# Attention's main loop given out as tasks by a list schedule, and k's parts carried across the rows by one transfer per head

## The chip, the cores and the metric

One core of a Trainium2 chip runs the whole program. The metric is the device time of one execution in microseconds. Its engines are PE (matmuls, with the weight loads shown apart as PEld), DVE (elementwise and reductions), ACT (activations and copies), POOL, and SP, which here only issues transfers.

## The reference

Attention with talking heads over 4 batches, 12 heads, 448 positions and 64 columns, then a mixture of experts (8 experts, one for each token) and an MLP with h * cos(h). The change touches attention alone:

```python
scores = scale * np.matmul(q, k.transpose(0, 1, 3, 2))
scores = np.einsum('bhij,hg->bgij', scores, w_pre)
scores = scores - np.max(scores, axis=-1, keepdims=True)
attn = np.exp(scores)
attn = attn / (np.sum(attn, axis=-1, keepdims=True) + 1e-09)
attn = np.einsum('bhij,hg->bgij', attn, w_post)
return np.matmul(attn, v)
```

All inputs are float32, and w_in and w_out of the MLP arrive as 64-bit words that the program turns into float32 itself.

## The kernel before

Attention walks over 4 batches. Each batch has 4 chunks of rows (120, 120, 120 and 88), so there are 16 chunks X. A chunk is cut into 12 or 9 blocks, 180 blocks n in all, 45 for each batch. A block holds up to 10 rows with all 12 heads, one row and head to a partition.

For each chunk and head, `qk` makes a score with two matmuls (L170 and L171: k's high part and low part against qs, which has q's high part in one half of the rows and its low part in the other). The scores go from PSUM to a tile S (L43 is the copy on ACT, L45 the one on DVE). For each block, `relay` has SP bring its rows out of S into a tile x (L191). `premix` multiplies x by the mixing matrix kpre into m (L196), DVE takes the row maximum nm (L198) and ACT the exponential E with its sum (L201). `scale` is three short DVE operations (L210, L211, L213) that give kr, the second mixing matrix divided by the sums. `postmix` is four matmuls of E against kr into pa (L223), which is copied to AT. When a chunk is complete, `av` multiplies AT by v (L237, px, copied to xc), `rows` transposes the result (L296, pt, copied to xr, stored by SP), and every fourth chunk or so the gate's logits (L266) and the routing's counts (L568 to L596) follow.

While a batch runs, the heads of the next one are prepared: `load_qk` loads k and q, `turned` transposes a pair of heads on PE (L89), `split_k1` and `split_q1` take the high part on ACT (L100, L121) and the low part on DVE (L101, L122). Scores read k's parts from all 128 rows, but a head's transpose fills only 64 of them. So `split_k1` copies them across: the high part on POOL (L102), the low part on POOL for batch 0 (L104) and on DVE for the others (L106).

Beside this runs the side job `narrow64`: 64 pieces of w_in and w_out. A piece is loaded by SP (L1313, W), squared on ACT (L1317, sq), put together by four DVE operations (L1322 to L1325, f) and stored by SP (L1328). Only the MLP at the end of the program reads the results.

The loop over blocks states the work in one order; which copy goes to ACT and which to DVE is decided by `Balance`, which adds up estimated costs. The order in which each engine and SP then run the loop's instructions is not the written one: outside a `manual_schedule` the compiler's own scheduler orders them by its priorities and its cost model. Each engine runs its instructions strictly in the order that results. Behind the loop, `between` works off the last chunk's products beside the first expert, in a written order.

Of the kernel before, what the change touches and what calls it, by code (L numbers as in the profile page):

```python
# [11 lines left out]
F32 = mybir.dt.float32  # L12
F32R = mybir.dt.float32r
# [14 lines left out]
ROUTE = (1, 8)  # L28
# [3 lines left out]
class Balance:  # L32
# [6 lines left out]
    def copy(self, out, in_, n):  # L39
        a, d = 0.19 + n * 0.00083, 0.07 + n * 0.00104  # L40
        if self.act + a <= self.dve + d:
            self.act += a
            return self.nc.scalar.copy(out, in_)  # L43
        self.dve += d
        return self.nc.vector.tensor_copy(out, in_)  # L45


def attention(ctx, qctx, tc, q, k, v, w_pre, w_post, wg, xs, lg, ident, nb=4, side=None, route=None):
# [45 lines left out]
    def split_k1(b, j, i, ps):  # L94

        h = 2 * j + i
        kh = ok.tile([128, S], F32R, tag=f"KH{h}", name=f"KH{b}_{h}")
        kl = ok.tile([128, S], F32R, tag=f"KL{h}", name=f"KL{b}_{h}")
        r, o = HALF[i], HALF[1 - i]
        nc.scalar.copy(kh[r], ps[r, :S])  # L100
        nc.vector.tensor_tensor(kl[r], ps[r, :S], kh[r].bitcast(F32), op=ALU.subtract)  # L101
        nc.gpsimd.tensor_scalar(kh[o], kh[r].bitcast(F32), 1.0, 0.0, op0=ALU.mult, op1=ALU.add)  # L102
        if b == 0:
            nc.gpsimd.tensor_scalar(kl[o], kl[r].bitcast(F32), 1.0, 0.0, op0=ALU.mult, op1=ALU.add)  # L104
# [258 lines left out]
    for n in range(3):  # L363
        relay(n)
    nxt = [1, 0]
    for n in range(N + 2):
        if n < N:
            X, be = blocks[n]
            b, c = chunks[X]
            nblk = CH[c][2]  # L370
            if n + 3 < N:
                relay(n + 3)

            if X + 1 < len(chunks):
                due = min(H, math.ceil(H * (be + 1) / (nblk - 3)))
                while nxt[0] == X + 1 and nxt[1] < due:
                    qk(X + 1, nxt[1])
                    nxt[1] += 1
                if nxt[0] == X + 1 and be == nblk - 1:
                    nxt = [X + 2, 0]  # L380
            premix(n)

            if b + 1 < nb:
                turn = (c - 2) * 12 + be - 2
                if c == 1 and be in (6, 7, 8):
                    load_qk(b + 1, be - 6)
                for j in range(H):
                    if turn == j * 5 // 4:
                        (split_q if j % 2 else split_k)(b + 1, j // 2)
                        if j in (1, 3, 5):  # L390
                            load_qk(b + 1, j // 2 + 3)
            if be == 2 and X > 0:
                av(X - 1)
            if route is not None and be in ROUTE:
                route.step()
            if be == 3 and c == 0 and X > 0:
                for g in range(4):
                    load_v(b, g)
            if be == 4 and X > 0:
                rows(X - 1)  # L400
            if be == 5 and X - 1 in GROUPS:
                logits_out(GROUPS[X - 1], logits_mm(GROUPS[X - 1]))
            if be == 6 and X - 1 in GROUPS:
                logit_tiles(X - 1)
        if n >= 2:
            postmix(n - 2)
        if n < N:
            scale(n)
        if side is not None:
            side()  # L410
            bal.dve += 0.6
            bal.act += 0.17
    if side is not None:
        side(True)
    if route is not None:
        route.step(True)
# [6 lines left out]
E = 8  # L423
# [867 lines left out]
def narrow64(ctx, tc, pairs, nblocks, bal=None):  # L1291
# [27 lines left out]
    def bits(i):  # L1319
        w, sq = W.pop(i), SQ.pop(i)  # L1320
        f = F[i] = wk.tile([P, C], I32, tag="f", name=f"f{i}")
        V.tensor_scalar(f, w[:, :, 1], 3, 0x3FFFFFFF, op0=ALU.logical_shift_left, op1=ALU.bitwise_and)  # L1322
        V.scalar_tensor_tensor(f, w[:, :, 0], 29, f, op0=ALU.logical_shift_right, op1=ALU.bitwise_or)
        V.scalar_tensor_tensor(f, w[:, :, 1], -0x40000000, f, op0=ALU.bitwise_and, op1=ALU.bitwise_or)
        V.scalar_tensor_tensor(f.bitcast(F32), sq, lim * lim, f.bitcast(F32), op0=ALU.is_ge, op1=ALU.mult)  # L1325
# [4 lines left out]
    stages = (store, bits, square, load)  # L1330
    state = [0, 0.0]

    def step(rest=False):
        state[1] += len(jobs) / nblocks
        while rest or state[1] >= 1:
            state[1] -= 1
            i = state[0]
            if i >= len(jobs) + 3:
                return
            for s, f in enumerate(stages):  # L1340
                j = i - (3 - s)
                if 0 <= j < len(jobs):
                    f(j)
            state[0] += 1

    return step
# [42 lines left out]
def kernel(ctx, tc, q, k, v, w_pre, w_post, w_gate, w1, w2, w_in, w_out, out):  # L1389
# [13 lines left out]
    with ExitStack() as cm:  # L1403
        with ExitStack() as c:
            with ExitStack() as cq:
                side = narrow64(c, tc, [(w_in, wi), (w_out, wo)], 170)
# [116 lines left out]
```

## Time and profile before

| | us |
|---|---|
| three timed runs | 1382.6, 1384.67, 1386.79 |
| median | 1384.67 |
| profiled execution, its own time | 1385.57 |
| its span, first to last instruction | 1383.9 |
| PE busy | 1325.9 |
| DVE busy | 1107.6 |
| ACT busy | 862.8 |
| POOL busy | 105.4 |

Matmuls are pipelined, and the profile models their ends, so the end of one overlaps the start of the next; start to start is the safer measure. In the tables of stretches each row gives the stretch, its length, then for PE, PEld, DVE, ACT and POOL the busy time with the number of instructions, the granted clock of PE as a share of full speed, the busy share of the 16 DMA engines and GB/s. In the lists of groups a row gives line, engine, operation, output<-input with their sizes and the count, then the busy time and the mean ns of one, then the idle time before them and what ended it. In the lists of waits a row gives who waited for whom, the total in us, how often, and the longest. In timelines: start, length, engine, line, operation, count.

### The profile page before, as it was taken

Reading aid. Unit: us, or ns where it says so; the run is one execution under the profiler, and the core shown is the slowest. Engines: PE = TensorE matmul, PEld = TensorE weight load, DVE = VectorE, ACT = ScalarE, POOL = GpSimd, SP = SyncE. Lnnn points to the kernel's source line nnn. Section 1 sums busy time; section 2 is a strip of 40 time slices with the busy share of each in tenths; the row PEclk is TensorE's granted clock in tenths of the full one; section 3 lists DMA queues with packets and bytes.
Section 4 is the critical chain, followed back from the end, with each engine's and each line's share of the span. In section 5 each row is a group of like instructions: output and inputs, shape, how many; then the busy total and the mean of one; then the engine's idle time right before and its main releaser. Section 6 shows DMA issues by size and latency. Waiting matters only on the chain.

```text
span 1383.9 us, 24811 instructions
## 1 busy us (share of the span) xinstructions
PE 1325.9 (96%) x8634; PEld 1103.8 (80%) x8634; DVE 1107.6 (80%) x2529; ACT 862.8 (62%) x1598; POOL 105.4 (8%) x127
## 2 busy tenths in 40 slices
PE   7888999899989999899999999999999999999997
PEld 5666777577767777789999999999888888888886
DVE  8789888998897766899999999899666666666663
ACT  7558656765685555788888888876444444444432
POOL 4001000100010000110001000001100010001001
PEclk9999999999999999999999999999999999999999
DMA  7866666676664337137835876166433343324201
GB/s 191 240 197 197 210 199 211 185 211 211 196 195 133 99 118 268 45 126 274 308 129 164 291 261 217 55 223 210 142 103 114 103 137 103 103 92 138 91 23 46
DMA packets 153281, 227.00 MB, mean 164 GB/s; under 512 B 55744, under 2 KB 115392, under 8 KB 153152
## 3 DMA queue, kind: packets, MB, share of 16 engines
q1 hardware_dynamic: 146816, 200.20, 45.9%
q0 software_dynamic: 3744, 18.09, 3.9%
q10 hardware_dynamic: 2592, 7.08, 1.3%
q8 instruction: 70, 1.15, 0.4%
q14 instruction: 59, 0.48, 0.1%
HBM read 217.87 MB, written 31.85 MB: 180 GB/s over the span
## 4 chain that ended last, share of the span: by engine, by line
PE 57%; issue 0%; DVE 0%; POOLq 0%; ACT 0%; POOL 0%
PE dh L1255 17%; PE op L1199 17%; PE yp L1014 10%; PE h L980 10%; PE ph L1001 1%; PE px L908 1%; PE dpt L1136 1%; POOLq L1518 0%; POOL out_dram L1208 0%; ACT dhs L1259 0%; ACT r L1222 0%; PE gspg L757 0%; DVE r L1220 0%; DVE r L1219 0%; PE pc L793 0%
## 5 line engine op out<-in xcount | busy, mean ns | idle before, releaser
L820 DVE TENSOR_TENSOR wl<-r,wh 128x768 fp32r<-128x768 f32 (+1 forms) x246 | 249.0, 1061 | 12.3 <-ACT wh L819 9.4
L819 ACT CAST wh<-r 128x768 fp32r<-128x768 f32 (+1 forms) x246 | 224.1, 931 | 38.4 <-PE h L980 30.2
L223 PEld LDWEIGHTS pa<-kr,E 120*112 120x112 f32 (+1 forms) x1440 | 168.6, 177 | 59.1 <-issue 26.5
L223 PE MATMUL pa<-kr,E 120*112 120x120 f32 (+1 forms) x1440 | 185.7, 270 | 9.0 <-DVE kr L213 5.6
L196 PE MATMUL m<-x,kpre 120*120 120x448 f32 x360 | 167.2, 548 | 7.0 <-ACT E L201 7.0
L820 DVE TENSOR_TENSOR wil<-wi,wih 128x768 fp32r<-128x768 f32 x64 | 60.9, 953 | 133.9 <-ACT wih L819 133.9
L201 ACT ACTIVATE E<-m,nm 120x448 f32<-120x448 f32 x180 | 114.1, 634 | 70.0 <-DVE nm L198 50.6
L819 ACT CAST wih<-wi 128x768 fp32r<-128x768 f32 x64 | 53.7, 841 | 158.9 <-PE dh L1255 158.0
L198 DVE TENSOR_REDUCE nm<-m 120x1 f32<-120x448 f32 x180 | 110.8, 616 | 9.5 <-PE m L196 8.5
L1199 PE MATMUL op<-woh,gh 128*128 128x512 f32 x448 | 115.2, 338 | 0.0
L1199 PE MATMUL op<-woh,gl 128*128 128x512 f32 x448 | 114.6, 336 | 0.0
L1199 PE MATMUL op<-wol,gh 128*128 128x512 f32 x448 | 114.4, 336 | 0.0
L1255 PE MATMUL dh<-dxh,wih 128*128 128x512 f32 (+1 forms) x384 | 112.8, 369 | 0.0
L1255 PE MATMUL dh<-dxl,wih 128*128 128x512 f32 (+1 forms) x384 | 112.4, 367 | 0.0
L1255 PE MATMUL dh<-dxh,wil 128*128 128x512 f32 (+1 forms) x384 | 111.6, 367 | 0.0
L170 PE MATMUL s<-KH,QS 128*120 128x448 f32 (+1 forms) x192 | 87.6, 456 | 13.0 <-DVE S L45 4.9
L819 ACT CAST woh<-wo 128x768 fp32r<-128x768 f32 x64 | 53.3, 834 | 53.4 <-PE op L1199 51.8
L237 PEld LDWEIGHTS px<-AT,vn 112*64 112x64 f32 x1536 | 75.2, 137 | 8.8 <-ACT AT L43 5.8
L237 PE MATMUL px<-AT,vn 112*64 112x120 f32 (+1 forms) x1536 | 80.9, 261 | 1.1 <-ACT AT L43 0.9
L43 ACT COPY S<-s 120x448 f32<-120x448 f32 (+1 forms) x147 | 75.6, 530 | 9.6 <-PE s L171 8.9
L1255 PEld LDWEIGHTS dh<-dxl,wih 128*128 128x128 f32 x384 | 70.2, 189 | 13.1
L1255 PEld LDWEIGHTS dh<-dxh,wil 128*128 128x128 f32 x384 | 69.8, 189 | 13.1
(263 smaller groups left out, 2723.7 us busy)
## 6 DMA issues: line engine op xcount, KB each, us to landing
r<-in_moe_w_dram SPq DMA_DIRECT2D x54, 1024.0 KB
r<-in_moe_w_dram SPq DMA_DIRECT2D x72, 768.0 KB
x<-S SPq DMA_DIRECT2D x172, 210.0 KB
wi<-wi SPq DMA_DIRECT2D x32, 768.0 KB
wo<-wo SPq DMA_DIRECT2D x32, 768.0 KB
W<-in_moe_w_in_dram SPq DMA_DIRECT2D x32, 384.0 KB
W<-in_moe_w_out_dram SPq DMA_DIRECT2D x32, 384.0 KB
ys<-y ACTq DMA_DIRECT2D x17, 384.0 KB
```

Source lines behind the costliest of these rows:

```text
L170: nc.tensor.matmul(ps[:n, :S], QS[b, h][:, i0 : i0 + n], KH[b, h], start=True, stop=False)
L196: nc.tensor.matmul(ps[:M, :S], kpre[:M, :M], XR.pop(n)[:M], start=True, stop=True)
L198: nc.vector.reduce_max(nm[:M], ps[:M, :S], axis=AX.X, negate=True)
L201: last["act"] = nc.scalar.activation(e[:M], ps[:M, :S], AF.Exp, bias=nm[:M], scale=1.0, accum_out=sg[:M])
L223: nc.tensor.matmul(pa[:112, c, :120], e[:M, c * 112 : c * 112 + 112], kr[:M], start=True, stop=True)
L237: nc.tensor.matmul(px[64 * e : 64 * e + 64, pr, :n], VN[b, g // 3][:, g % 3, cc], AT[X][:, cc, g, :n], start=(cc == 0), stop=(cc == 3))
L819: self.latest["A"] = nc.scalar.copy(hi, src).ins
L820: self.latest["V"] = nc.vector.tensor_tensor(lo, src, hi.bitcast(F32), op=ALU.subtract).ins
L980: self.nc.tensor.matmul(hp[n], a[:, k], w[:, n * 512 : n * 512 + 512], start=(k == 0 and i == 0), stop=(k == 5 and i == 2))
L1014: self.nc.tensor.matmul(yp[n][:, :384], a[:, k], w[:, n * 384 : n * 384 + 384], start=(k == 0 and i == 0), stop=(k == 7 and i == 2))
L1199: nc.tensor.matmul(bank[:, to], g[:, t * P : t * P + P], w[:, of], start=first, stop=(f == 15 and i == 2), skip_group_check=(n == 1))
L1255: nc.tensor.matmul(hp[:, :N], w[:, k], x[:, k, :N], start=(k == 0 and i == 0), stop=(k == 5 and i == 2))
```

## The change

The loop over blocks is gone. Its work is written as tasks, Python generators that yield a step at a time: which engine it runs on and for how long (two numbers: how long the engine is held, how long until the result is there), which buffers it takes and gives back, and which events of other tasks it waits for. A task is a block, the score of a chunk and head, a pair of heads of k or of q, the loads of v, the products of a chunk, the logits of a group with their routing, or a piece of the side job. Each has a rank. `Plan.run` takes, again and again, the step that can start first, and among steps of the same engine that can start within 0.02 us the one of the lowest rank, and emits its instructions at once. A copy that may run on either engine is offered on both. The pieces of the side job are marked `bg`: one is passed over where a step that is not goes first, and their ranks are spread over the loop from 4 to 171 in steps of 170/64. The durations in the steps are numbers like those of a trace. All of it stands in a `manual_schedule` that includes SP, so each engine and SP keep the order in which the plan emitted.

The scores of a batch's last chunk are given a rank 8 blocks earlier than those of others.

k's parts are now the two halves of one tile K of 128 x 2 x 448. For the batches behind the first, POOL issues one transfer per head that copies the 64 rows of both parts to the other 64 rows; POOL's copy of the high part and DVE's copy of the low part (L106) are gone. Batch 0 still has POOL's two copies.

```diff
-        kh = ok.tile([128, S], F32R, tag=f"KH{h}", name=f"KH{b}_{h}")
-        kl = ok.tile([128, S], F32R, tag=f"KL{h}", name=f"KL{b}_{h}")
+        both = ok.tile([128, 2, S], F32R, tag=f"K{h}", name=f"K{b}_{h}")
+        kh, kl = both[:, 0], both[:, 1]
...
-            nc.vector.tensor_copy(kl[o], kl[r].bitcast(F32))
-            bal.dve += 0.3
+            nc.gpsimd.dma_start(out=both[o], in_=both[r])
...
-    for n in range(N + 2):
...
+    def dve(d):
+        return {"DVE": (d - 0.07, d)}
+    def copying(n):
+        return {"ACT": (0.05 + n * 0.00092, 0.12 + n * 0.00092), "DVE": (n * 0.00124, 0.07 + n * 0.00124)}
...
+    def block(n):
+        yield dict(run=dma(4.2), take=["x"], on=[("S", X, h) for h in range(H)], ends=[("x", n)])
+        relay(n)
+        yield dict(run=pe(0.752), take=["m"], reached=n)
...
+        yield dict(run=pe(0.82), later=0.5, take=["o"] + (["AT"] if be == 0 else []), on=[("post", n - 1)] if n else [], ends=[("post", n)])
...
+    for n in range(N):
+        plan.add(n, block(n))
+    for X in range(1, len(chunks)):
+        n0, nb0 = first_of[X], CH[chunks[X - 1][1]][2]
+        for h in range(H):
+            plan.add(n0 - 3 - 8 * (X % 4 == 3) - (H - 1 - h) * (nb0 - 4) / H, score(X, h))
...
+    if side is not None:
+        count, *ops = side
+        for i in range(count):
+            plan.add(4 + i * 170 / count, piece(i, *ops), bg=True)
+    with tc.manual_schedule(engines=START | {mybir.EngineType.SP}):
+        plan.run()
```

What this does to DVE's order is seen near the end of batch one, where heads of the next batch are prepared. Before (L106 is the copy of k's low part, L1324 and L1325 are operations of the side job, L198, L210, L211 and L213 the block's maximum and scaling, L101 and L122 the low parts of k and q):

```order
L211 RECIPROCAL rs_1800<-rs_1800 120x1
L1324 SCALAR_TENSOR_TENSOR f_2529<-W_2289,f_2529 128x384
L106 CAST KL_8_1783<-KL_8_1783 64x448
L101 TENSOR_TENSOR KL_9_1789<-tp_4_0_0_1777,KH_9_1788 64x448
L213 TENSOR_SCALAR kr_1803<-kpost,rs_1800 120x120
L106 CAST KL_9_1789<-KL_9_1789 64x448
L210 TENSOR_SCALAR rs_1839<-sg_1820 120x1
L198 TENSOR_REDUCE nm_1866<-m_1864 120x1
L211 RECIPROCAL rs_1839<-rs_1839 120x1
L1325 SCALAR_TENSOR_TENSOR f_2529<-sq_2422,f_2529 128x384
L122 TENSOR_TENSOR QS_8_1827<-tp_4_1_0_1822,QS_8_1827 64x448
L213 TENSOR_SCALAR kr_1842<-kpost,rs_1839 120x120
```

Now, at the same work (L487 is the maximum, L494, L496 and L499 the scaling, L546 and L555 the low parts, L1563 the side job's first operation):

```order
L487 TENSOR_REDUCE nm_1713<-m_1673 120x1
L496 RECIPROCAL rs_1711<-rs_1711 120x1
L494 TENSOR_SCALAR rs_1719<-sg_1682 120x1
L555 TENSOR_TENSOR QS_6_1715<-tp_3_1_0_1703,QS_6_1715 64x448
L499 TENSOR_SCALAR kr_1727<-kpost,rs_1711 120x120
L496 RECIPROCAL rs_1719<-rs_1719 120x1
L487 TENSOR_REDUCE nm_1734<-m_1695 120x1
L555 TENSOR_TENSOR QS_7_1729<-tp_3_1_0_1703,QS_7_1729 64x448
L499 TENSOR_SCALAR kr_1746<-kpost,rs_1719 120x120
L546 TENSOR_TENSOR K_7_1744<-tp_3_0_0_1661,K_7_1744 64x448
L494 TENSOR_SCALAR rs_1766<-sg_1722 120x1
L1563 TENSOR_SCALAR f_1750<-W_1679 128x384
```

The copies L106 are gone, and the side job's operations stand further apart.

On PE the second place is the border before the third chunk of batch three, from its last score (s_11) on. Before:

```order
L171 MATMUL s_11_4788<-KL_11_3724,QS_11_3819 120x448
L196 MATMUL m_4792<-x_4688,kpre 120x448
L568 LDWEIGHTS tri
L568 MATMUL pq_4810<-ohb,tri 128x8
L570 LDWEIGHTS ones
L570 MATMUL pq_4810<-ohs,ones 128x8
L223 MATMUL pa_4827<-kr_4744,E_4726 112x120 x4
L196 MATMUL m_4840<-x_4712,kpre 120x448
L223 MATMUL pa_4847<-kr_4784,E_4766 112x120 x4
L196 MATMUL m_4870<-x_4756,kpre 120x448
L223 MATMUL pa_4877<-kr_4836,E_4796 112x120
L596 LDWEIGHTS Le_4821
```

There follow a premix, two scores and a postmix before the first premix that reads the new chunk. Now, from the same score:

```order
L522 MATMUL s_11_4843<-K_11_3825,QS_11_3712 120x448
L523 MATMUL s_11_4843<-K_11_3825,QS_11_3712 120x448
L505 MATMUL pa_4847<-kr_4840,E_4818 112x120 x4
L522 MATMUL s_5_4853<-K_5_3518,QS_5_3487 88x448
L523 MATMUL s_5_4853<-K_5_3518,QS_5_3487 88x448
L484 MATMUL m_4859<-x_4690,kpre 120x448
L522 MATMUL s_6_4864<-K_6_3554,QS_6_3515 88x448
L523 MATMUL s_6_4864<-K_6_3554,QS_6_3515 88x448
L484 MATMUL m_4874<-x_4713,kpre 120x448
L522 MATMUL s_7_4882<-K_7_3645,QS_7_3528 88x448
L523 MATMUL s_7_4882<-K_7_3645,QS_7_3528 88x448
L181 MATMUL tp_0_0_0_4888<-ident,kn_0_3772 128x112 x4
```

One more score follows, then the first premix of the new chunk. Scores of the batch's last chunk (of 88 rows) and transposes for the next batch have come in between, and less work lies between the last score and that premix.

## Rows read from the trace of the kernel before

**Rows 1.** The page: engines over the span, PE's 40 slices, an issue of POOL.

```profile
PE 1325.9 (96%) x8634; PEld 1103.8 (80%) x8634; DVE 1107.6 (80%) x2529; ACT 862.8 (62%) x1598; POOL 105.4 (8%) x127
...
PE   7888999899989999899999999999999999999997
...
wpp<-in_w_pre_dram POOLq DMA_DIRECT2D x1, 0.6 KB, 3.2
```

**Rows 2.** Instructions on tile x: durations min/median/max, first and last start.

```profile
L196 PE MATMUL m<-x,kpre x360: 537/539/954, 28.6 to 553.0; 120*120 120x448 f32 x172, 108*108 108x448 f32 x8
L191 SPq DMA_DIRECT2D x<-S x180: 768/801/1127, 24.2 to 543.2; - x180
```

**Rows 3.** Stretches: the four batches and the whole main loop.

```profile
28.60:161.20 132.60, 118.70 (x883) 88.32 (x882) 116.12 (x330) 89.12 (x212) 7.07 (x12) 0.99 0.69 206
161.20:301.90 140.70, 128.59 (x1063) 98.06 (x1062) 125.84 (x384) 89.73 (x215) 7.69 (x12) 0.99 0.69 204
301.90:437.50 135.60, 127.37 (x1068) 96.71 (x1067) 120.72 (x383) 89.57 (x213) 7.27 (x12) 1.00 0.62 189
437.50:557.10 119.60, 118.25 (x1053) 91.78 (x1052) 79.96 (x317) 65.54 (x165) 1.27 (x2) 1.00 0.50 163
28.60:557.10 528.50, 492.90 (x4062) 374.88 (x4061) 442.64 (x1412) 333.96 (x803) 23.31 (x38) 0.99 0.63 191
```

**Rows 4.** Timeline of PE in three short stretches.

```profile
501.64 0.92 PE L196 MATMUL m<-x,kpre 120*120 120x448 f32 x2
502.39 0.98 PE L223 MATMUL pa<-kr,E 120*112 120x120 f32 x8
503.14 0.44 PE L170 MATMUL s<-KH,QS 128*88 128x448 f32 x1
...
503.62 0.92 PE L196 MATMUL m<-x,kpre 120*120 120x448 f32 x2
...
296.90 0.98 PE L223 MATMUL pa<-kr,E 120*112 120x120 f32 x8
297.72 0.92 PE L196 MATMUL m<-x,kpre 108*108 108x448 f32 x2
...
263.76 0.57 PE L89 MATMUL tp<-ident,kn 112*128 112x112 f32 x4 [0.60 <-PE tp L89]
264.18 1.00 PE L223 MATMUL pa<-kr,E 120*112 120x120 f32 x8
```

**Rows 5.** Groups of instructions in the main loop, 28.6 to 557.1 us.

```profile
L237 PE MATMUL px<-AT,vn 112*64 112x120 f32 (+1 forms) x1440 | 77.0, 262 | 1.0 <-ACT AT L43 0.9
L296 PE MATMUL pt<-ident,xc 128*120 128x128 f32 (+1 forms) x90 | 13.0, 278 | 0.0
L266 PE MATMUL pl<-xc,wgs 128*8 128x120 f32 (+1 forms) x180 | 7.0, 261 | 0.0
...
L43 ACT COPY S<-s 120x448 f32<-120x448 f32 (+1 forms) x146 | 75.1, 530 | 9.6 <-PE s L171 8.9
L106 DVE CAST KL<-KL 64x448 fp32r<-64x448 f32 x36 | 14.3, 398 | 1.1
```

**Rows 6.** Waits in the main loop.

```profile
ACT E L201 <- DVE nm L198: 50.6, 67, 4.1
ACT sq L1317 <- DMA W<-in_moe_w_in_dram: 27.5, 18, 3.1
...
PE m L196 <- ACT E L201: 7.0, 11, 1.0
```

**Rows 7.** The same stretches, DVE's operations on tile f alone.

```profile
28.60:161.20 132.60, 44.83 (x90) 0.99 0.69 206
...
437.50:557.10 119.60, 0.00 (x0) 1.00 0.50 163
sum 528.50, DVE 128.22; mean DVE 32.06
```

**Rows 8.** Waits of SP's queue in the main loop.

```profile
SPq L1313 <- DVE f L1324: 41.8, 26, 3.2
```

More of the change, by code (lines that the diff above doesn't have):

```diff
@@ L362, in attention @@
     N = len(blocks)
-    for n in range(3):
-        relay(n)
-    nxt = [1, 0]
-    for n in range(N + 2):
-        if n < N:
-            X, be = blocks[n]
-            b, c = chunks[X]
[L370 to L412, printed above, removed]
@@ L413, in attention, with pe, act @@
-    if side is not None:
-        side(True)
-    if route is not None:
-        route.step(True)
+    first_of = {X: n for n, (X, be) in reversed(list(enumerate(blocks)))}
+    end_of = {X: n for n, (X, be) in enumerate(blocks)}
+    A, V, G = nc.scalar.copy, nc.vector.tensor_copy, nc.gpsimd
+    by = {"ACT": A, "DVE": V}
+    def pe(d):
+        return {"PE": (d, d + 0.17)}
+    def dve(d):
+        return {"DVE": (d - 0.07, d)}
+    def act(d):
+        return {"ACT": (d - 0.07, d)}
+    def copying(n):
+        return {"ACT": (0.05 + n * 0.00092, 0.12 + n * 0.00092), "DVE": (n * 0.00124, 0.07 + n * 0.00124)}
@@ new lines, in score @@
+    def score(X, h):
+        b, c = chunks[X]
+        i0, rows_, _ = CH[c]
+        on = [("K", b, h), ("Q", b, h)]
+        if X >= 2:
+            on += [("x", k) for k in range(first_of[X - 2], end_of[X - 2] + 1)]
+        if h:
+            on.append(("s", X, h - 1))
+        yield dict(run=pe(0.46), take=["q"], on=on, ends=[("s", X, h)])
+        if h == 0:
+            SB[X] = sk.tile([120, H, S], F32, tag="Sb", name=f"S{X}")
+        ps = pq.tile([128, 512], F32, tag="q", name=f"s{X}_{h}")
+        nc.tensor.matmul(ps[:rows_, :S], QS[b, h][:, i0 : i0 + rows_], KH[b, h], start=True, stop=False)
+        nc.tensor.matmul(ps[:rows_, :S], QS[b, h][:, i0 : i0 + rows_], KL[b, h], start=False, stop=True)
+        eng = yield dict(run=copying(S), later=-2, give=["q"], ends=[("S", X, h)])
+        by[eng](SB[X][:rows_, h], ps[:rows_, :S])
@@ new lines, in values, with products @@
+    def values(b):
+        for g in range(4):
+            yield dict(run=dma(3.5), on=[("av", 4 * b - 1, 0), ("av", 4 * b - 1, 1)], ends=[("V", b)] if g == 3 else [])
+            load_v(b, g)
+    def products(X):
+        n = CH[chunks[X][1]][1]
+        b = chunks[X][0]
+        ats = [("AT", k) for k in range(first_of[X], end_of[X] + 1)]
+        for half in range(2):
+            yield dict(run=pe(0.02 * n + 0.21), on=ats + [("V", b)], take=["v"] + (["xc"] if half == 0 else []), give=["AT"] if half else [], ends=[("av", X, half)])
+            px = av_mm(X, half)
+            eng = yield dict(run=copying(3 * n), give=["v"], ends=[("xc", X)] if half else [])
+            av_out(X, half, px, by[eng])
+        for half in range(2):
+            yield dict(run=pe(0.33), take=["v"] + (["xr"] if half == 0 else []))
+            pt = rows_mm(X, half)
+            eng = yield dict(run=copying(384), give=["v"])
+            rows_out(X, half, pt, by[eng])
+        yield dict(run={"none": (0.0, 3.0)}, give=["xr"])
@@ L417, in attention @@
+    for X in range(len(chunks) - 1):
+        plan.add(end_of[X] + 3, products(X))
+    for last_, Xs in GROUPS.items():
+        plan.add(end_of[last_] + 5, gates(Xs))
+        for X in Xs:
+            plan.add(end_of[last_] + 5, freed(X))
+    if side is not None:
+        count, *ops = side
[3 more added lines that the diff above has]
+        plan.run()
     return SimpleNamespace(
@@ L1288, in run, with narrow64 @@
                 part2(item, tiles)
-def narrow64(ctx, tc, pairs, nblocks, bal=None):
+def narrow64(ctx, tc, pairs):
     nc = tc.nc
```

210 lines of the change are left out of this document (189 added, 21 removed).

## The prediction

> **What bounds the kernel now.** First the page's engine shares and slices: PE is busy for 96% of the span, with 7 to 9 tenths up to the eighteenth slice and 9 behind it [rows 1], so a change pays only where PE idles, in the first part. The loose stretch is attention's main loop, from the first premix at 28.6 us [rows 2] to 557.1, its 180 blocks in four batches of 45. The table of stretches cuts it at the batches' first premixes [rows 3]. Batches one to three take 132.6, 140.7 and 135.6 us, with DVE busy for 116 to 126 of each and PE idle for 8 to 14. Batch four takes 119.6, with DVE at 80.0 and PE at 118.2. The granted clock is 0.99 to 1.00 throughout and is no part of this.
>
> How much of PE's busy time is work? The timeline of PE gives start to start, free of the modelled ends [rows 4]: premix 0.75 (501.64 to 502.39), postmix 0.75 before a score (502.39 to 503.14) and 0.82 before a premix (296.90 to 297.72), the two matmuls of a score 0.48 (503.14 to 503.62), four turned pieces 0.42 (263.76 to 264.18). So 180 premixes are 135 us, 180 postmixes at 0.785 (half of each kind, my assumption) 141, 177 scores 85, 36 turns 15; the products with v 77.0, their transposes 13.0 and the logits 7.0 by their busy time [rows 5], and the routing about 10 (an estimate: 13 tiles with four short matmuls each, at most 52 by the 0.278 of a transpose). The sum is 483 us of work in 528.5, or 91%. Batch four alone: 45 blocks 69, 36 scores 17, four of the window's 15 products 20.5, a quarter of transposes, logits and routing 7.5: 114 of 119.6, or 95%. Batches one to three are the other 369 in 408.9, or 90%. That gap is what a better order can win, and the chip has already run the better rate in batch four.
>
> Who is late? In the waits [rows 6] the exponentials on ACT wait 50.6 us for the row maxima of DVE, and ACT stands 27.5 us before squares of the side job whose W has not landed. PE itself waits most for ACT's exponentials, which hold the banks of the premix. Cause: DVE carries the side job early. Its operations on f take 128.2 us, 44.8 of them in batch one and none in batch four [rows 7].
>
> **The change part by part.**
> 1. The copy of k's low part on DVE goes: 36 of 398 ns, 14.3 us [rows 5], all in batches one to three. So do 36 POOL copies of k's high part; POOL is busy for 23.3 of the 528.5 us [rows 3] and heads are made long before they are read, so I count 0 for them.
> 2. In their place POOL issues 36 transfers of both parts. The trace has no such transfer; the nearest POOL row is w_pre, which lands 3.2 us after its issue, but with 0.6 KB [rows 1]; the nearest in size is x, 210 KB against 224, which is issued at 24.2 us and used at 28.6, so at most 4.4 us [rows 2]. In the new order some 14 us of PE's work (7 postmixes, 4 premixes, 11 scores) lie between the last head's transfer (K_11) and its score, and more for the other heads. From either row the price is 0; with the cover gone, each us of lateness would cost up to 1 us for each of 3 batches, as the last head alone is late. Its 8 MB more go beside a DMA share of 0.50 to 0.69 [rows 3]; price 0, at worst what rival 4 has.
> 3. The side job's pieces are spread over the loop. In the new order of DVE 16, 17, 17 and 14 pieces lie in the four batches, against about 22.4, 20.9, 20.9 (the mean of what is left) and 0. A piece is 128.2/64 = 2.0 us. With step 1, a third of it each, DVE goes to about 116.1-4.8-12.8 = 98, 125.8-4.8-7.8 = 113, 120.7-4.8-7.8 = 108, and 80.0+28 = 108. Early, DVE then has slack; in batch four it has 108 of some 118 us and takes the slack away.
> 4. Which copy goes to ACT and which to DVE is chosen by the plan. Counted over the loop it hardly alters: AT has 73 copies on DVE instead of 66, S 30 instead of 34, xc 3 instead of 12. Seven copies more against thirteen fewer, all of one kind of size: taken as 0.
> 5. The order of all engines and of SP is set by durations near the chip's. This is the largest term, and no row has its price. From below: the first three batches stay as they are, and only step 1 counts; DVE is not always what PE waits for, so 0 to 14 us. From above: PE never waits, 528.5-483 = 45.5 us. The nearest row is batch four: its 95% for the whole loop gives 483/0.95 = 508.4 us, 20 us less. That stage got there with an order made on other durations; batches one to three come close to its DVE slack, batch four loses it. I take a sixth of the way from 508.4 to 483, 504 us: 24.5 us less.
> 6. At the chunks' borders the first premix of a chunk needs its last score copied and brought by SP: 0.53 for ACT's copy [rows 5] and 4.4 for x, 5 us. PE's work between the two was 6.2 to 7.4 us; now it is 4.6 to 7.9 at eleven borders and over 15 at the others, and three are below 5. Up to 0.4 each makes 1 us, and is in the 504.
>
> Sum: the profiled execution took 1385.6 us, 1.7 beside its span; less 24.5 it is 1361, and its like in the three timed runs, whose median is 0.9 lower, 1360 us. Behind 557.1 nothing changes: the experts' instructions come in nearly the same order, and the MLP, which reads the side job's results, comes after all experts.
>
> **A rule against the row.** Matmul busy time leaves 528.5-492.9 = 35.6 us to win [rows 3]. The Trainium skill, Perfetto Trace Analysis, section Identifying the Most-Contended Engine, says that matmul occupancy is a bad measure of headroom and the busy share of weight loads a good one. By that rule the loads' 374.9 us in 528.5, or 71%, leave far more. The trace sides with it in part: in batch four PE is 98.9% busy by matmuls and the loads are at 91.8/119.6 = 76.7%. If the whole loop came to that share, it would take 374.9/0.767 = 489 us, 40 us less; that is rival 1.
>
> **The rivals.**
> 1. PE is kept full: loads at batch four's share all through, 489 us for the loop, 1385.6-40-0.9 = 1345. For it: ACT is at 63% and DVE at 84% of the loop, so both have room. Against it: batch four must now carry 28 us of side work, and PE, DVE and ACT are coupled three times in each block.
> 2. The order gains little and mostly step 1 counts, with part of the even spread: 5 to 14 us, 1370 to 1380. For it: DVE's total falls by only 14 of 443 us.
> 3. No gain: PE's waits are those of the chain premix, maximum, exponential, kr, postmix, which stays as long as it was; 1384. Against it: with the same DVE share, batch three has PE at 94% and batch one at 90%.
> 4. Slower: SP is now held to the written order. Stores of f and loads of W stand between the x transfers, each waits for DVE, and all x queued behind wait too; before, loads of W alone held SP for DVE 41.8 us in 26 waits [rows 8], hidden by the 6 to 7 us at the borders. If x comes L later than 4.4 us at the 15 borders, it costs 15 L less the slack. At L = 3 that is up to 45, less 24.5: 1405. At no slack it decides from L of about 1.6, where 15 L is the 24.5. The W and f of 14 pieces now also meet the experts' weights in batch four.
>
> **How the numbers follow.** Forecast 0.52 (loop 498 to 511, that is 1354 to 1367), rival 1 0.16, rival 2 0.16, rival 3 0.06, rival 4 0.10. A measurement of this kernel tells a change from none at about 0.3%, 4 us. Faster is then 0.84, same 0.06, slower 0.10. The range reaches from 43 us less, 1341, to 5 us less, 1380; it leaves out rivals 3 and 4 and the end of rival 1.
>
> **What would show it.** Right: batches one to three at 122 to 132 us each, batch four at 117 to 121; DVE at 98 to 112 in each; ACT's waits for W nearly gone and those for the maxima well below 50 us; no wait of PE for x or K. Wrong: loads of PE idle time released by a DMA or by SP (rival 4), the same idle shares beside an even DVE (rival 3), or DVE above 90% in every batch with PE waiting for it (rival 2).

## The result, and the profile after

The changed kernel takes 1404.05 us (median of 4 runs, 1399.3 to 1405.76), the kernel before beside it 1383.83: a ratio of 1.0137, 95% interval 1.0112 to 1.0163. That is 20 us slower, where 24 us faster was forecast. The profiled execution took 1403.67 us, its span is 1401.7.

The page after, in the parts of [rows 1]: PE, DVE and POOL over the span, PE's slices, DMA's slices, the software and hardware queues, and the new transfer with its median time to landing.

```profile
PE 1333.9 (95%) x8634; PEld 1110.6 (79%) x8634; DVE 1089.4 (78%) x2487; ACT 868.3 (62%) x1604; POOL 104.5 (7%) x127
...
PE   7996999889978999999999999999999999999996
...
DMA  7669765977695759227844686166533343324201
...
q1 hardware_dynamic: 146816, 200.20, 47.0%
q0 software_dynamic: 6624, 26.35, 6.9%
...
K<-K POOLq DMA_DIRECT2D x36, 224.0 KB, 6.7
```

DVE has 18 us less to do, 14.3 of them the copies that went, but PE's busy time rose by 8 us with the same 8634 matmuls, and a transfer lands 6.7 us after its issue.

The stretches after, cut at the first premixes of the batches, answering to [rows 3]:

```profile
30.40:166.85 136.45, 123.31 (x994) 93.83 (x992) 106.55 (x300) 85.91 (x203) 6.32 (x12) 0.97 0.74 192
166.85:314.65 147.80, 135.73 (x1121) 103.71 (x1119) 111.81 (x349) 91.46 (x217) 6.11 (x12) 0.93 0.74 193
314.65:456.65 142.00, 128.01 (x1009) 97.93 (x1007) 110.62 (x357) 89.57 (x211) 6.11 (x12) 0.95 0.72 191
456.65:571.50 114.85, 112.44 (x941) 85.73 (x938) 95.62 (x365) 69.02 (x172) 1.74 (x2) 1.00 0.77 243
30.40:571.50 541.10, 499.49 (x4057) 381.20 (x4056) 424.61 (x1370) 335.95 (x802) 20.29 (x38) 0.96 0.74 203
```

The loop went from 528.5 to 541.1 us. Batch four, which prepares no next batch, is 5 us shorter; batches one to three are 4, 7 and 6 us longer, with the granted clock at 0.93 to 0.97 instead of 0.99 to 1.00. The other 5 of the 18 us between the two spans lie outside: the first premix comes 1.8 us later, and what follows the loop takes 830.2 us instead of 826.8. Where inside the batches? This table, worked out from the starts of the 180 premixes, says how many us later (+) a block starts than in the kernel before:

```
block    15     35     40     45     60     80     85     90    125    130    135    160    179
after  -10.3  -12.6  -11.1   +5.6   -5.5  -12.3   -7.9  +12.8   -1.6   +1.6  +19.2  +15.2  +14.6
```

Each batch runs ahead of the old order and loses it all in its last ten blocks: 17 to 21 us at each of the three borders (blocks 45, 90, 135). Part of the lead is lent and goes back anyway: the kernel with copies on POOL (below), which hardly idles there, also gives back 12 us at block 45 (-17.8 to -6.0). But there the next batch's heads are turned, split and carried. Three stretches of 45 us hold most of them, first in the kernel before, then after (columns as in [rows 3]: PE, PEld, DVE, ACT, POOL busy, clock, DMA share, GB/s):

```profile
110.00:155.00 45.00, 40.56 (x308) 30.40 (x309) 42.35 (x109) 35.09 (x81) 5.91 (x10) 1.00 0.66 189
250.00:295.00 45.00, 40.49 (x306) 30.25 (x307) 42.87 (x110) 33.98 (x79) 6.19 (x10) 1.00 0.68 189
395.00:440.00 45.00, 42.29 (x320) 32.17 (x319) 41.15 (x112) 32.86 (x77) 5.00 (x8) 1.00 0.45 141
```

```profile
110.00:155.00 45.00, 33.80 (x265) 25.63 (x265) 32.61 (x85) 25.03 (x57) 4.69 (x9) 0.92 1.05 213
250.00:295.00 45.00, 34.55 (x232) 25.75 (x231) 30.20 (x78) 23.68 (x54) 4.58 (x9) 0.77 0.97 196
395.00:440.00 45.00, 34.03 (x248) 26.04 (x247) 29.58 (x80) 24.70 (x57) 4.58 (x9) 0.85 0.85 179
```

Before, DVE was the busiest beside PE in these stretches (41 to 43 of 45 us). After, every engine is idler, and the DMA share is 0.85 to 1.05 (it adds up the packets' times, so by this count it can pass 1) for hardly more bytes: 213 GB/s instead of 189 in the first stretch. What PE waits for there is in its timeline (start, us, instruction, in brackets the idle time before it):

```profile
122.65 0.98 PE L484 MATMUL m<-x,kpre 120*120 120x448 f32 x2 [2.20 <-DMA x<-S]
123.47 0.98 PE L505 MATMUL pa<-kr,E 120*112 120x120 f32 x8
125.94 0.57 PE L181 MATMUL tp<-ident,qn 112*128 112x112 f32 x4 [1.49 <-DMA qn<-in_q_dram]
126.36 0.99 PE L505 MATMUL pa<-kr,E 120*112 120x120 f32 x8
131.68 0.98 PE L181 MATMUL tp<-ident,kn 112*128 112x112 f32 x4 [4.34 <-DMA kn<-in_k_dram]
132.45 1.71 PE L484 MATMUL m<-x,kpre 120*120 120x448 f32 x2
```

PE waits for loads, of x, q and k, and when it goes on after 4.3 us of idling the premix pair takes 1.71 us instead of 0.92: the clock has been lowered. In slices of 10 us the granted clock is 0.93 from 120 to 130 us, where PE is busy for 3.65, and 0.73 in the next; a granted clock below 1 is a mean of the two levels, 1.2 and 2.4 GHz. The waits over the loop, answering to [rows 6] and [rows 8]:

```profile
ACT E L491 <- DVE nm L487: 17.0, 19, 1.4
...
PE tp L181 <- DMA kn<-in_k_dram: 15.7, 5, 4.3
...
ACT sq L1557 <- DMA W<-in_moe_w_in_dram: 11.5, 6, 5.1
...
PE tp L181 <- DMA qn<-in_q_dram: 7.4, 5, 2.6
...
PE m L484 <- ACT E L491: 6.0, 9, 1.9
...
PE m L484 <- DMA x<-S: 3.2, 2, 2.2
...
SPq L1570 <- DVE f L1566: 28.7, 13, 8.7
```

The old waits shrank: those for the maxima from 50.6 to 17.0 us, as forecast, and those for W of w_in from 27.5 to 11.5, which is not the "nearly gone" of the forecast. SP's longest wait for f is now at its store, 28.7 us. New waits of PE took their place: 26 us behind loads. For K its scores are listed with 0.5 us in all.

### The profile page after: what moved, and what is told of

Its sections match the earlier page's. It is cut to its first block, busy times and chain, and to the rows that moved or that the text cites. A ratio compares the mean times of both kernels' runs of the same rounds, so it can differ in the third digit from the quotient of the medians.

```text
span 1401.7 us, 24741 instructions
## 1 busy us (share of the span) xinstructions
PE 1333.9 (95%) x8634; PEld 1110.6 (79%) x8634; DVE 1089.4 (78%) x2487; ACT 868.3 (62%) x1604; POOL 104.5 (7%) x127
## 4 chain that ended last, share of the span: by engine, by line
PE 56%; issue 0%; DVE 0%; POOLq 0%; POOL 0%; ACT 0%
PE dh L1495 17%; PE op L1439 17%; PE yp L1254 10%; PE h L1220 10%; PE ph L1241 1%; PE px L1148 1%; PE dpt L1376 1%; POOLq L1744 0%; POOL out_dram L1448 0%; ACT dhs L1499 0%; PE gspg L997 0%; DVE r L1459 0%; DVE r L1460 0%; PE pc L1033 0%; DVE u L1457 0%
## 5 line engine op out<-in xcount | busy, mean ns | idle before, releaser
L1059 ACT CAST wh<-r 128x768 fp32r<-128x768 f32 (+1 forms) x246 | 224.0, 931 | 38.2 <-PE h L1220 30.6
L505 PEld LDWEIGHTS pa<-kr,E 120*112 120x112 f32 (+1 forms) x1440 | 172.6, 181 | 39.7 <-issue 16.9
L484 PE MATMUL m<-x,kpre 120*120 120x448 f32 x360 | 171.9, 564 | 10.2 <-ACT E L491 6.0
L487 DVE TENSOR_REDUCE nm<-m 120x1 f32<-120x448 f32 x180 | 111.5, 620 | 26.3 <-PE m L484 22.8
L522 PE MATMUL s<-K,QS 128*120 128x448 f32 (+1 forms) x180 | 94.0, 522 | 4.7 <-ACT S L525 3.3
L525 ACT COPY S<-s 120x448 f32<-120x448 f32 (+1 forms) x151 | 79.0, 532 | 24.2 <-PE s L523 22.1
L508 ACT COPY AT<-pa 112x480 f32<-112x480 f32 (+1 forms) x107 | 60.6, 567 | 33.5 <-PE pa L505 32.3
```

The lines of the kernel that those rows point to most:

```text
L484: nc.tensor.matmul(ps[:M, :S], kpre[:M, :M], x[:M], start=True, stop=True)
L487: nc.vector.reduce_max(nm[:M], ps[:M, :S], axis=AX.X, negate=True)
L505: nc.tensor.matmul(pa[:112, c, :120], e[:M, c * 112 : c * 112 + 112], kr[:M], start=True, stop=True)
L522: nc.tensor.matmul(ps[:rows_, :S], QS[b, h][:, i0 : i0 + rows_], KH[b, h], start=True, stop=False)
L1059: self.latest["A"] = nc.scalar.copy(hi, src).ins
```

## The experiments

Ratios are to the kernel before, timed on the same chip, with 95% intervals. Lines of code are those of the changed kernel unless said otherwise. The steps' durations enter the plan, so a kernel whose steps change gets an order of its own. In the traces only the kernel without the rounded type runs in the changed kernel's order, and only the two with idle transfers in that of the kernel with both copies on POOL. "New order" below means an order made by the plan, "old order" one made by the compiler's scheduler, which also orders each kernel anew.

**The transfer, in four doses.** The first four kernels ask whether the transfers or the new order lose the time. With copies on the engines in place of the transfer:

```diff
-                yield dict(run={"POOL": (0.75, 4.0)}, ends=[("K", b, h)])
-                nc.gpsimd.dma_start(out=both[o], in_=both[r])
+                yield dict(run={"POOL": (0.61, 0.67)})
+                nc.gpsimd.tensor_scalar(kh[o], kh[r].bitcast(F32), 1.0, 0.0, op0=ALU.mult, op1=ALU.add)
+                yield dict(run={"DVE": (0.33, 0.4)}, ends=[("K", b, h)])
+                nc.vector.tensor_copy(kl[o], kl[r].bitcast(F32))
```

> The changed kernel with its plan, but k's two parts are again copied across the rows by engines (high part on POOL, low part on DVE, planned at 0.61 and 0.33 us) and not by a transfer. Theory A (the 36 transfers of 224 KB saturate the DMA engines while heads are prepared, and loads of k and q and x come late): DMA share in the stretches around 115-160, 255-300 and 400-440 us falls from 0.85-0.95 to about 0.7, PE's waits for the loads of k and q (23 us in the changed kernel) shrink to under 5, the 17 to 20 us lost at each batch border go, the granted clock rises from 0.982 to 0.99, time about 1365 us although DVE has 14 us more. Theory B (the plan starts the heads too late and too tightly, transfer or not): borders still lose 10 us or more each, time 1390 to 1405.

Measured: 1379.86 us, ratio 0.9971 (0.9958 to 0.9984). With the copies of before on POOL and DVE the new order is worth 4 us, and the transfers cost 24 over that. The list of PE's waits has no load of k or q any more.

Half the bytes: the high part copied on POOL as above, only the low part sent.

```diff
+                yield dict(run={"POOL": (0.61, 0.67)})
+                nc.gpsimd.tensor_scalar(kh[o], kh[r].bitcast(F32), 1.0, 0.0, op0=ALU.mult, op1=ALU.add)
...
-                nc.gpsimd.dma_start(out=both[o], in_=both[r])
+                nc.gpsimd.dma_start(out=kl[o], in_=kl[r])
```

> The changed kernel, with k's high part copied on POOL and only the low part carried by the transfer, so each of the 36 transfers has 112 KB instead of 224. Theory A: about half of the loss at the borders is left, time 1375 to 1390, median landing of the transfer under 6.7 us. Theory B: as the changed kernel, 1395 to 1405.

Measured: 1395.01 us, 1.0072 (1.0045 to 1.0100). Half the bytes cost 15 us over the copies on POOL and DVE (1380), and 27 over those on POOL alone (1368, below): more than half. The time lies above theory A's range and at the lower edge of theory B's.

The heads ranked eight blocks earlier, transfers as they are:

```diff
-                plan.add(first_of[4 * b] - 18 + j + 0.5 * s_, heads(b, j, s_))
+                plan.add(first_of[4 * b] - 26 + j + 0.5 * s_, heads(b, j, s_))
```

> The changed kernel with the rank of the heads' tasks 8 blocks earlier (first_of - 26 instead of - 18); in the order the last head's transpose then stands some four blocks earlier. The transfers stay. Theory A: the DMA engines are as full as before while heads are prepared, loads still come late, and the cover of other blocks behind hides part: 1385 to 1400. Theory B: the next batch's scores no longer wait for the heads, the borders lose under 5 us each, 1355 to 1370.

Measured: 1391.90 us, 1.0056 (1.0037 to 1.0074): 12 of the 24 us back, but no gain over before. The transfers are not spread further: the 12 of a batch are issued within 53 to 57 us, as against 56 to 62. But they and the loads come some three to six blocks earlier, and PE's waits for loads of k, 15.7 us in the changed kernel, are 2.4 here.

The transfer alone, in the kernel before, with its own order:

```diff
-        kh = ok.tile([128, S], F32R, tag=f"KH{h}", name=f"KH{b}_{h}")
-        kl = ok.tile([128, S], F32R, tag=f"KL{h}", name=f"KL{b}_{h}")
+        both = ok.tile([128, 2, S], F32R, tag=f"K{h}", name=f"K{b}_{h}")
+        kh, kl = both[:, 0], both[:, 1]
...
-            nc.vector.tensor_copy(kl[o], kl[r].bitcast(F32))
-            bal.dve += 0.3
+            nc.gpsimd.dma_start(out=both[o], in_=both[r])
```

> The kernel before, with its own order, where only the copies of k's parts for batches behind the first are replaced by one POOL transfer per head. Theory A: the transfers meet the loads of heads here too, slower than before: 1390 to 1420. Theory B: DVE loses 14 us of copies and nothing waits: 1370 to 1385.

Measured: 1415.80 us, 1.0218 (1.0182 to 1.0255). The transfers cost 32 us in an order in which the new planner has no part. What PE waited for in this order is less clear: its longest waits are for copies on ACT and for x, and no load of k or q is among them. Theory A's ranges hold in the last two kernels only; B's holds, at its edge, in the one with half the bytes. Against B speaks that taking out the transfers gives 24 us with a plan of the same kind, and that they cost as much where there is no plan. But A missed the size of the first kernel by 15 us: without transfers the new order should have given 19. Something else held it.

**What the transfers do.** The same transfers from SP's hardware queue, and on POOL's queue without the rounded type:

```diff
-                yield dict(run={"POOL": (0.75, 4.0)}, ends=[("K", b, h)])
-                nc.gpsimd.dma_start(out=both[o], in_=both[r])
+                yield dict(run=dma(4.0), ends=[("K", b, h)])
+                nc.sync.dma_start(out=both[o].bitcast(F32), in_=both[r].bitcast(F32))
```

> The same 36 transfers of 224 KB, issued by SP on its hardware queue instead of by POOL on the software queue; nothing else is changed but the planner's entry for the engine. Theory A1 (what costs is the bytes, whichever queue carries them): 1398 to 1408, as the changed kernel, DMA share again 0.9 to 1.1 in the head stretches. Theory A2 (what costs is the software queue, whose packets of 3584 bytes take 299 ns each): the share falls below 0.9 there and the time to 1380 to 1392, near the kernel with engine copies (1380). Rival A3 (SP now waits in order for DVE's low part before each transfer, and the loads behind it are late): above 1408.

Measured: 1397.24 us, 1.0096 (1.0063 to 1.0129), between A1 and A2 and nearer to A1. Its first head stretch:

```profile
110.00:155.00 45.00, 35.47 (x288) 26.56 (x286) 35.44 (x96) 28.95 (x67) 0.00 (x0) 1.00 0.99 212
```

The DMA share stays at 0.99. PE idles here nearly as in the changed kernel, but the clock keeps at 1.00; over the loop PE is busy for 491.6 us instead of 499.5. This is the fastest of five executions: it took 1393 us at a clock of 0.994 over the span, the other four 1396 to 1401 at 0.983 to 0.987, beside 0.979 to 0.984 in the changed kernel. So the clock at 1.00 belongs to this execution and not to the kernel. The queue is at most a small part of the cause: 7 of the 36 us, with an order that changed too.

```diff
-                nc.gpsimd.dma_start(out=both[o], in_=both[r])
+                nc.gpsimd.dma_start(out=both[o].bitcast(F32), in_=both[r].bitcast(F32))
```

> The same 36 transfers on the same POOL queue, with both sides read as plain float32 instead of the rounded float32 type. Theory A4 (the type makes the transfer a converting one, and that is what is slow): the landing falls from 6.7 us to under 5 and the time to 1380 to 1395. Theories A1 and A2: no change, 1400 to 1408, landing 6.5 to 7.

Measured: 1406.32 us, 1.0138 (1.0088 to 1.0188), landing 6.7 us, in the same order. The type is nothing; A4 falls.

**What held the engine copies.** In their kernel the head stretches look so:

```profile
110.00:135.00 25.00, 18.09 (x121) 12.59 (x121) 23.27 (x56) 16.59 (x35) 5.02 (x8) 0.86 0.74 188
240.00:270.00 30.00, 23.39 (x163) 16.53 (x162) 28.49 (x71) 20.04 (x47) 5.41 (x9) 0.89 0.76 199
375.00:400.00 25.00, 20.07 (x103) 13.11 (x102) 24.06 (x63) 17.49 (x40) 3.38 (x6) 0.86 0.73 199
```

DVE is busy for 93 to 96% of them and PE for 72 to 80%. So two kernels that were to have less DVE work in these blocks, by ranking the heads earlier and by moving the copies:

```diff
-                plan.add(first_of[4 * b] - 18 + j + 0.5 * s_, heads(b, j, s_))
+                plan.add(first_of[4 * b] - 26 + j + 0.5 * s_, heads(b, j, s_))
```

> The kernel with engine copies in place of the transfers (1380), with the heads of the next batch ranked 26 blocks ahead of it instead of 18. Theory D (without the transfers the head stretches are bound by DVE, which is busy 9.2 to 9.7 of 10 us there while PE is at 6.3 to 8.1): the same DVE work is spread over more blocks, and the time falls to 1368 to 1376. Rival (the order costs elsewhere what it gives there: premixes that wait for E): 1378 to 1388.

Measured: 1374.27 us, 0.9936 (0.9910 to 0.9962), some 6 us less and in theory D's range. But the same work is not spread over more blocks: the heads' turns lie in 14 or 15 blocks, as against 15 to 17, only earlier. So D's reason is not shown by this run.

```diff
-                yield dict(run={"DVE": (0.33, 0.4)}, ends=[("K", b, h)])
-                nc.vector.tensor_copy(kl[o], kl[r].bitcast(F32))
+                yield dict(run={"POOL": (0.61, 0.67)}, ends=[("K", b, h)])
+                nc.gpsimd.tensor_scalar(kl[o], kl[r].bitcast(F32), 1.0, 0.0, op0=ALU.mult, op1=ALU.add)
```

> The kernel with engine copies (1380), with both copies on POOL (busy 8% of the span), none on DVE: 36 copies of 0.39 us leave DVE's head stretches. Theory D (DVE bounds these stretches): 14 us less of DVE's work in three stretches, of which PE gets 6 to 12, so 1368 to 1376. Rival (the chain by a head gets longer by 0.2 us of POOL, or DVE slows beside a busy POOL): 1378 to 1388.

Measured: 1367.97 us, 0.9874 (0.9829 to 0.9918). That is at the lower edge of theory D's range and clear of the rival's, so D stands here. This kernel has a plan like the change's and DVE's relief, without the transfers: its loop, and its first head stretch,

```profile
30.80:538.30 507.50, 485.08 (x4059) 371.02 (x4058) 428.65 (x1367) 336.78 (x807) 45.90 (x74) 1.00 0.66 200
...
110.00:155.00 45.00, 40.91 (x354) 31.67 (x354) 39.07 (x103) 33.45 (x76) 9.50 (x15) 1.00 0.67 184
```

The loop is 21 us shorter than before, and 33.6 shorter than the changed kernel's: 14.4 of these are PE's own time (499.5 against 485.1), 19.2 are PE idle. The 14.4 are the clock's: by the trace's clock records PE is busy at the lower level for 30.6 us of the changed loop and for 2 us of this one, and half the difference is 14.3.

**Traffic or lateness?** The kernel with POOL's copies again, with transfers that nothing waits for, to DRAM and then within SBUF:

```diff
+                nc.gpsimd.dma_start(out=aside[12 * b - 12 + h], in_=both[r])
...
+    aside = dram.tile([36, 64, 2, 448], F32R, name="aside")
```

> The kernel with both of k's copies on POOL (1368), and besides them one transfer of 224 KB per head on POOL's queue, of the same two rows, to a scratch place in DRAM that nothing reads: the traffic of the changed kernel, without anything that waits for it. Theory T (the traffic costs, by making the loads of k, q and x late while the heads are prepared): 1383 to 1400, DMA share 0.9 or more in the stretch from 110 to 155 us. Rival L (the latency costs: k's lower row comes 6 to 7 us after its parts are ready, and the chain by head gets longer): 1366 to 1373, with the added transfers on the queue but PE not waiting for kn, qn or x.

Measured: 1379.29 us, 0.9970 (0.9955 to 0.9985): 11 us more than without, short of what T said and above what L said. The DMA share from 110 to 155 us is 0.76, not the 0.9 of T.

```diff
-    LT = cp.tile([8, 2 * S], F32, name="LT")
+    LT = cp.tile([128, 2 * S], F32, name="LT")
+    aside = cp.tile([128, 704], F32, name="aside")
...
+                to = (aside[64:], aside[:64], LT[64:, :704])[h % 3]
+                nc.gpsimd.dma_start(out=to, in_=both[r].rearrange("p a s -> p (a s)")[:, :704].bitcast(F32))
```

> As the kernel with the idle transfer to DRAM (1379), but the transfer goes within SBUF, to three places that nothing reads: 36 transfers of 176 KB (704 of 896 columns, since no more room is left), on POOL's queue, and k itself copied on POOL. In the changed kernel the packets of the loads beside the transfers took 25 ns (256 bytes) and 124 ns (1792 bytes) instead of 18 to 21 and 84 to 86; beside the idle transfer to DRAM they took 19 and 85. Theory S (a transfer within SBUF slows the packets beside it, and most of the 36 us between 1368 and 1404 comes by that): packets of 23 to 25 ns, 1385 to 1400. Rival L (what is left of the 36 us is the late k itself and the plan made for it): 1372 to 1383, whatever the packets do.

Measured: 1393.14 us, 1.0072 (1.0053 to 1.0092): 25 us more than without, by traffic alone, in the same order and with 79% of the bytes. Rival L falls. The loops of the two, that to DRAM first:

```profile
30.35:547.60 517.25, 492.98 (x4059) 378.01 (x4058) 429.38 (x1367) 337.47 (x807) 66.70 (x110) 0.98 0.70 212
...
29.90:562.10 532.20, 497.84 (x4059) 379.26 (x4058) 429.59 (x1367) 336.90 (x807) 66.45 (x110) 0.97 0.72 203
```

Against the loop without them (507.5, PE busy for 485.1) the first has 7.9 us more of PE's busy time and 1.9 more of its idle time, the second 12.8 and 11.9. With the transfers within SBUF PE waits for k's loads, which it did not do in the kernel it was made from (waits of PE, whole span):

```profile
PE tp L181 <- DMA kn<-in_k_dram: 12.6, 4, 4.4
```

The packets show part of why. The mean time of a packet by size, from the trace's packet records between 110 and 155 us (256 bytes are those of k's and q's loads, 1792 those of x):

```
kernel                              256 B    1536 B   1792 B   3584 B (transfer)
before                              18 ns    68 ns     83 ns      -
copies on POOL                      21       68        86         -
  + idle transfer to DRAM           19       69        85       218 ns
  + idle transfer within SBUF       24       71       111       420 (5632 B)
after                               25       90       124       300
after, on SP's queue                28       83       109       238
```

Beside transfers within SBUF the packets of loads and of x are 1.1 to 1.6 times as long; beside one that reads the same rows and writes DRAM they are not. The same records say how long a load takes. With the 256-byte packets in order of time and 448 of them to a load, this is the time from a load's issue to the end of its last packet, over the 64 loads of k and q issued behind 90 us:

```
kernel                              median us    longest
before                                2.3          3.7
copies on POOL                        2.6          4.3
  + idle transfer to DRAM             3.4          5.6
  + idle transfer within SBUF         4.3          9.0
after                                 5.2          9.8
after, on SP's queue                  3.8          7.1
the transfer in the old order         3.3          8.2
```

So the loads do land late, but not by the length of their own packets: 448 packets on 16 engines are 28 each, and 4 to 7 ns on each is 0.1 to 0.2 us (an estimate), where 2.6 are missing. They also land later beside the transfer to DRAM, where no packet is longer. Most of a load's time must pass between its packets; what passes there, and why a target in SBUF costs more than one in DRAM, no run separates. The Trainium skill, SBUF — State Buffer, section Door 1: The DMA port swizzle, says that DMA bandwidth depends on how many of SBUF's 16 DMA ports the partitions reach, and by its formula rows 0 to 63 reach one half of them and rows 64 to 127 the other; transfers that all write 64 rows would then crowd 8 ports. No run here changed the number of rows, so that is not shown.

**Two more.** Both remedies together, copies on POOL and heads 26 blocks ahead:

> Both copies on POOL, and the heads ranked 26 blocks ahead instead of 18. Theory D (DVE bounds the head stretches also now, busy 9.3 to 9.6 of 10 us from 100 to 130 us): 1360 to 1366. Rival (with DVE relieved there is nothing left to spread, and E is late in the blocks between, as with the transfers, where earlier heads gave 12 us): 1367 to 1373.

Measured: 1365.97 us, 0.9875 (0.9856 to 0.9894), not to be told from the 1367.97; the rival's range begins at 1367, theory D's reaches to 1366. It beats both kernels of this study: 1.2% under before and 2.7% under the changed one.

And the kernel before in its own order, its low parts copied on POOL:

```diff
-        if b == 0:
-            nc.gpsimd.tensor_scalar(kl[o], kl[r].bitcast(F32), 1.0, 0.0, op0=ALU.mult, op1=ALU.add)
-        else:
-            nc.vector.tensor_copy(kl[o], kl[r].bitcast(F32))
-            bal.dve += 0.3
+        nc.gpsimd.tensor_scalar(kl[o], kl[r].bitcast(F32), 1.0, 0.0, op0=ALU.mult, op1=ALU.add)
```

> The kernel before, in its own order, with k's low part copied on POOL instead of DVE, so that only the 14.3 us of DVE copies go and nothing else changes. Theory D (DVE bounds the head stretches of the old order too): 1370 to 1379. Rival (the old order spreads the heads so that the copies were beside other work, and only the new order's crowded heads make DVE the bound): 1381 to 1386.

Measured: 1378.50 us, 0.9963 (0.9944 to 0.9982), as theory D said. More than the copy changed: `Balance` is no longer charged for it and gives DVE 40 copies of S instead of 33 and 14 of xc instead of 10, so that DVE's busy time in the loop falls from 442.6 to 435.6 us, by half of the 14.3. The six main kernels then make a table (medians, us):

```
k's lower row by        old order    new order
POOL and DVE copies      1384         1380
POOL copies alone        1379         1368
the transfer             1416         1404
```

Each column says the same of the transfer (+32 and +24 against the old copies, +37 and +36 against POOL's), the rows of the order -4, -11 and -12. The first two rows do not compare equal work on DVE, as the loops of the new order with the copies of before and of the old order with POOL's show:

```profile
30.00:546.50 516.50, 492.08 (x4055) 375.27 (x4054) 447.65 (x1420) 330.18 (x789) 23.49 (x38) 0.98 0.65 196
...
28.56:551.60 523.04, 493.79 (x4064) 377.58 (x4063) 435.63 (x1388) 329.16 (x791) 48.06 (x74) 0.99 0.62 193
```

In the new order DVE is busy for 447.7 us in the loop with the copies of before and for 428.7 with POOL's, where the plan also gives it 55 copies of AT instead of 66. So 19.0 us less on DVE gained 12 in the new order, and 7.0 less gained 4 to 5 in the old one, about 0.6 for each. At equal work on DVE the order would then be worth some 6 to 7 us in both rows, by an estimate from these numbers.

## Why the prediction was wrong

The step that failed is step 2, the transfers at a price of 0. It priced their landing (3.2 to 4.4 us) against the work between a transfer and its score, and that part was not what failed: they land after 6.7 us and PE is not seen waiting for K. What failed is the sentence on their traffic: "Its 8 MB more go beside a DMA share of 0.50 to 0.69". The share itself was not too low a mean: where the heads are prepared it was 0.66, 0.68 and 0.45 before, no higher. But the transfers come there, 9 of a batch's 12 in 45 us, and with them the share rose to 1.05, 0.97 and 0.85. Their own packets make 0.24 of that in the first stretch (576 of 300 ns over 16 engines, an estimate), and the longer packets of the others about the rest. There k's and q's loads landed 2.6 us later in the median than with POOL's copies, up to 9.8 us after their issue; PE waited 26 us for loads, and its clock fell. The price of the step, DVE's relief apart, was 36 us. The idle transfer within SBUF shows 25 of them as traffic alone; whether the other 11 are the bytes that it lacks, the changed plan or the late k, no run separates.

Rival 4 gave almost the measured time, 1405, but not by its mechanism. It looked for x late at all 15 borders because SP stands behind stores of f; PE waits for x only 3.2 us, and loses the time at the three borders between batches. Nor do SP's waits for f explain it: at the stores of f they are 112 us in the loop, and 96 in the kernel with POOL's copies, which is 36 us faster. That the number came out is luck; of this rival only the sign, PE idle behind a DMA, was right.

Step 5, the new order, was right in kind, once the transfers are taken out, and too large: the loop was forecast at 504 us, and the kernel with POOL's copies has 507.5, but its gain in the medians was 16 us instead of 24.5, just outside the forecast's range. By the table most of that hangs on DVE's copies, and by the estimate behind it the order alone is worth 6 to 7 us. The prediction counted DVE by batches (98, 113, 108, 108; measured after: 106.6, 111.8, 110.6, 95.6). That hid where it is full: in the head stretches it was busy for 91 to 95% already before, and for 93 to 96% in the new order with the same copies. The new order does not crowd the heads: their turns lie in 14 blocks before a border in the old order, and in 15 to 17 in that one.

Step 1, DVE's copies: 14.3 us of busy time were bounded by "0 to 14"; in the old order taking them from DVE is worth 4 to 5, in the new one 12, with the shifts of other copies told above. Step 3 came as read from the order, as the f operations show, against [rows 7]:

```profile
30.40:166.85 136.45, 32.21 (x64) 0.97 0.74 192
...
456.65:571.50 114.85, 28.08 (x56) 1.00 0.77 243
30.40:571.50 541.10, 128.47 (x256) 0.96 0.74 203
```

Batch four took the 28 us of it and still fell from 119.6 to 114.9, below the 117 to 121 of the forecast. How much of that is owed to work done ahead, in the border that lost 18 us, was not separated. Step 4, taken as 0, was 3.7 us of DVE's time: 18.0 us less in the loop, 14.3 of them the copies. Step 6 is in the noise of this: PE's waits at scores for copies of S are 3.3 us in all. "Behind 557.1 nothing changes" missed the 3.4 us there; the kernel with POOL's copies has 0.3, and the cause stays open.

That the granted clock "is no part of this" held for the trace of before only. In the changed kernel it fell in the stretches where PE idled, and PE's slower work added 14 us to 19 of idling.

The list of what would show the prediction wrong named PE's idle time "released by a DMA", as rival 4's sign, and that is what the trace shows.

## What to carry to other kernels

Price a transfer in the stretch in which it runs, by the DMA share that its own packets add there and by what else is on the way: here PE waited 26 us for loads that came late beside the copies of k, and half a microsecond for the copies. Two copies of 0.6 us for each head, on an engine that is 8% busy, were worth 36 us against a transfer that looked free. Look at the busiest engine where the extra work lies and not over the batch: DVE, at 84% of the loop, was at 91 to 95% there. And where the order is made by a planner or a compiler, count what else it moved before a difference is put down to the edit.

## What the runs showed of the hardware that was not expected

- Beside transfers within SBUF, 64 rows to 64 rows, other packets take longer: 256 bytes 24 to 28 ns instead of 18 to 21, 1792 bytes 109 to 124 ns instead of 83 to 86; beside transfers of the same source to DRAM they take as long as without.
- Loads of 112 KB land later beside either: 2.6 us in the median without transfers, 3.4 beside those to DRAM, 4.3 beside those within SBUF.
- A transfer of 224 KB within SBUF took 6.7 us to land in the changed kernel, 5.2 in the old order and, to DRAM, 4.3. The Trainium skill, DMA: Bandwidth & Descriptors, section Anatomy of one DMA — SWDGE (gpsimd) path, fits 2.0 us and 1 us for each 436 KB, an estimate of 2.5 us here; the measurements are all above it, beside other traffic.
- Near-equal idling, unequal clock, in one execution each: from 110 to 155 us PE was busy for 33.8 us at a granted 0.92 in the changed kernel and for 35.5 at 1.00 with SP's queue, whose four other executions had a lower clock over the span.
